# One pass for the gates and the second norm's vectors, smaller filling matmuls, and another written-out order, in a fused attention and feed-forward layer

## The chip, the cores and the metric

The kernel runs on one core of a Trainium2 chip. The core has a matrix engine (TensorE, in the profile PE, with its weight loads shown apart as PEld), a vector engine (VectorE, DVE), an activation engine (ScalarE, ACT), a general engine (GpSimd, POOL) and a queue engine (SyncE, SP) that issues most transfers. Work memory is SBUF; matmuls write to PSUM. The metric is the device time of one execution in microseconds (us); lower is better. The kernel before takes 171.2 us, the median of three runs (170.99 to 171.49).

## The reference

The input x has 2048 rows of 448 values. A small vector c gives six modulation vectors of 448 values; attention is local: a row looks at 8 earlier rows, two apart, in 16 heads of 28 values.

```
mod = silu(c) @ w_mod                       # 448 -> 6 x 448
sa, ca, ga, sb, cb, gb = mod
h = layernorm(x) * (1 + ca) + sa
x = x + ga * (local_attention(h, wqkv) @ wo)
h = layernorm(x) * (1 + cb) + sb
x = x + gb * (silu(h @ w1) @ w2)            # 448 -> 1792 -> 448
```

So the first norm needs sa and ca as soon as it runs. The gate ga is needed when the product with wo is formed (the kernel multiplies it into wo), sb and cb with the second norm, gb before the product with w2.

## The kernel before, in words

The 2048 rows go through in four chunks of 512 rows (`NC = 4`), 256 of each parity (`CP = 256`). For chunk k the steps are: first norm (`n1.k`), its transposition and modulation (`T`, `mod`), projection to queries and keys in four groups (`QKk.i.g`), to values (`Vb`), logits `Lb.par`, exponentials `exp`, masks, the product with the values `AVb`, its normalisation `onorm`, a transposing transfer `oTb`, the output projection `WOk.i`, the second norm `n2.k`, and the two feed-forward products `F1.k.i` and `F2.u`. Nine blocks b of 112 positions carry the attention.

Most products of 448 deep sums are cut in halves of 64 partitions, two of which run in the array at a time (`halves`, `duo`); a product therefore comes in two pieces of 6 and 8 matmuls, with a "turn" on POOL between.

Every step is an operation of a class `Plan`. `Plan` can order them itself by costs, but the fast path does not: `ORDER` is a long string of operation numbers, written out by hand or by a search, with a letter where an operation may run on ACT (`a`) or DVE (`v`). Operations are issued in exactly this order, and each engine runs its own ones in this order. The semaphores follow from the buffers that are shared. The scarce buffer is PSUM: four slots (`ps`) of two banks each. Two engines that read the same slot are put one behind the other.

The pieces that matter here:

- `warm_up` (L403): matmuls on a tile of zeros (`junk`) that nobody reads. Eight come first (`WARM`), then five pairs (`JUNK`), spread between the first transposes.
- `mod_cols` (L423): modulation vectors as columns, for one norm: 32 matmuls with a single moving column (L433), then two small DVE copies to `modc` (L436, L437). It is called for sa and ca (the first norm), and again for sb and cb (the second).
- `gate` (L443): one gate, spread over all 128 partitions: four matmuls of 448 columns (L450) with `screp`, which is silu(c) repeated 128 times (L421), then a copy to `gbc` (L453, ACT in this order). It is called for ga and for gb.
- `wo*g` (L879) multiplies ga into wo on DVE; two transfers on SP (L882, L883) then copy the halves of wo across partitions; the output projections wait for them. `w2*g` (L884) multiplies gb into w2 in seven steps.
- `Norm.on_pe` (L520): the first chunk's two half norms (`n1.00`, `n1.01`) are transposed on PE. Each takes one PSUM slot, four transposes per row tile (L529) and two modulation operations of two instructions each (L536 on ACT, L538 on DVE).
- `pad` (L564, L566): spreads the loaded weights of queries and keys, four operations.
- The loads of w_mod are issued in parts: columns 0 to 2D early, then 2D to 3D, 3D to 5D and 5D to 6D, each as two transfers.

The order on PE from the first values to the second output projection is, in names (a name that comes twice is a product's two pieces):

```
V0 V0 V1 L1.0 V1 QK1.0.1 QK1.0.0 L1.1 ... QK1 ... AV0 gate AV1 L2.0 V2 V2 V3 L2.1 V3
QK2.0.0 QK2.0.2 L3.0 QK2.0.0 QK2.0.2 AV2 WO0.0 L3.1 WO0.0 QK2.0.3 QK2.0.1 V5 ... AV3 V5 WO0.1
... QK3 ... WO1.0 V6 ... QK3.0.3 V8 QK3.0.3 mods gate AV4 F1.0.6 ...
```

Of the kernel before, what the change touches and what calls it, by code (L numbers as in the profile page):

```python
# [7 lines left out]
BF16 = mybir.dt.bfloat16  # L8
# [7 lines left out]
D = 448  # L16
# [4 lines left out]
KT = 4  # L21
K3 = D - 384
SP_ = 1024
# [13 lines left out]
WARM, JUNK = 8, 5  # L37
# [204 lines left out]
def layer(ctx, tc, io, safe):  # L242
# [45 lines left out]
    maskb = ct([128, 2, 128], "maskb")  # L288
    c4, sc4 = (both[0:KT, KT * 6 * D + 1024 + 128 * a:KT * 6 * D + 1152 + 128 * a] for a in range(2))
    scT = ct([128, KT], "scT")  # L290
    screp = ct([128, KT, 128], "screp")
    scratch = (both[:, KT * 6 * D + 512:KT * 6 * D + 512 + D], wqk3[:])
    modc = ct([128, 4, KT], "modc", F32)
    gbc = ct([128, 2, D], "gbc")
# [704 lines left out]
```

## Time and profile before

| | |
|---|---|
| median of the runs | 171.2 us (170.99 to 171.49) |
| the profiled execution | 171.64 us, of which the span of instructions is 169.9 us |
| PE busy | 162.0 us (95% of the span) |
| ACT busy | 114.5 us (67%) |
| DVE busy | 96.1 us (57%) |
| POOL busy | 33.2 us (20%) |
| transfers | 17.51 MB |

The span runs from the first to the last instruction; about 1.7 us of the execution lie around it. Times of the traces count from the span's start. A matmul row's duration is its whole passage through the array, and neighbours overlap: the distance between starts, which the chain of waits shows as time over count, is what a matmul costs in a stream.

### The profile page before, as it was taken

What the parts mean: (1) busy time and instruction counts of PE and PEld (TensorE: products, weight loads), DVE (VectorE), ACT (ScalarE), POOL (GpSimd) and SP (SyncE); (2) the same over time, 40 slices, a digit from 0 to 9 for tenths busy, and PEclk for the clock granted to TensorE, in tenths of its full rate; (3) what the DMA queues carried; (4) which work ended last, traced back from release to release, by engine and by line L of the source; (5) the groups of instructions that cost most, each with busy time, mean ns of one, the idle gap of its engine ahead of it and who ended that gap; (6) DMA issues with size and microseconds to landing.
All of it is one profiled execution on the core that took longest, in us unless ns stands there. A gap on an engine that the chain in (4) does not pass through costs nothing.

```text
span 169.9 us, 4812 instructions
## 1 busy us (share of the span) xinstructions
PE 162.0 (95%) x2015; PEld 83.9 (49%) x2015; DVE 96.1 (57%) x189; ACT 114.5 (67%) x163; POOL 33.2 (20%) x88
## 2 busy tenths in 40 slices
PE   7799999899999999999999999999999999999990
PEld 2258644545554564455644544655544444445450
DVE  4777999899979963895352577732473000000451
ACT  3148999999876889999878998662767862420000
POOL 7342424730502221132000205120150000000000
PEclk9959999999999999999999999999999999999999
DMA  4994448489979874022020030086008000000031
GB/s 142 289 326 165 99 94 314 78 202 242 176 185 252 177 198 106 0 66 46 20 54 0 4 90 22 2 112 178 6 10 224 0 4 0 0 4 0 38 136 64
DMA packets 32054, 17.51 MB, mean 103 GB/s; under 512 B 23896, under 2 KB 31640, under 8 KB 32024
## 3 DMA queue, kind: packets, MB, share of 16 engines
q1 hardware_dynamic: 31872, 16.90, 39.9%
q8 instruction: 17, 0.28, 0.7%
q10 hardware_dynamic: 152, 0.23, 0.5%
q14 instruction: 13, 0.11, 0.2%
HBM read 9.12 MB, written 1.84 MB: 64 GB/s over the span
## 4 chain that ended last, share of the span: by engine, by line
PE 75%; ACT 10%; DMA 6%; issue 3%; DVE 2%; POOL 1%; ACTq 0%; POOLq 0%
PE ps L791 25%; PE ps L808 22%; PE ps L627 7%; PE ps L753 6%; PE ps L638 5%; ACT p L678 4%; PE ps L730 4%; DMA wqk<-in_A_wqkv_dram 3%; PE ps L832 3%; PE ps L670 3%; DMA x_all<-in_A_x_dram 2%; ACT h L536 2%; ACT qk L630 1%; POOL rs L487 1%; ACT both L480 1%
## 5 line engine op out<-in xcount | busy, mean ns | idle before, releaser
L791 PE MATMUL ps<-h,w 64*128 64x512 bf16 x392 | 44.7, 376 | 0.0
L808 PE MATMUL ps<-w,both 64*128 64x448 bf16 x392 | 39.9, 349 | 0.0
L794 ACT ACTIVATE both<-ps 128x1024 bf16<-128x1024 f32 x28 | 27.3, 1023 | 13.9 <-PE ps L791 13.8
L678 ACT ACTIVATE p<-ps 128x896 bf16<-128x896 f32 (+1 forms) x36 | 31.5, 928 | 3.3 <-PE ps L670 3.2
L791 PEld LDWEIGHTS <-w 64*128 64x128 bf16 x392 | 19.5, 94 | 21.6
L808 PEld LDWEIGHTS <-both 64*128 64x128 bf16 x392 | 18.9, 94 | 17.7
L823 DVE TENSOR_TENSOR ot<-ps,x_all 128x896 bf16<-128x896 f32 x7 | 7.6, 1088 | 34.6 <-PE ps L808 34.3
L627 PE MATMUL ps<-h,wp 64*128 64x256 bf16 (+1 forms) x224 | 20.4, 323 | 0.6 <-ACT h L536 0.4
L627 PEld LDWEIGHTS <-wp 64*128 64x128 bf16 x280 | 13.9, 94 | 11.3 <-issue 1.1
L704 DVE TENSOR_TENSOR p<-p,maskb 128x1792 bf16<-128x1792 bf16 (+1 forms) x18 | 19.3, 1098 | 0.0
L768 DVE SCALAR_TENSOR_TENSOR x_all<-ps,x_all 128x448 bf16<-128x448 f32 x16 | 9.3, 618 | 9.7 <-PE ps L753 9.7
L487 POOL TENSOR_TENSOR rs<-rs,negh 128x2 f32<-128x2 f32 x16 | 13.8, 861 | 1.3
L753 PE MATMUL ps<-wo,oT 64*128 64x448 bf16 x112 | 13.0, 350 | 0.0
L480 ACT ACTIVATE wqk<-x_all,mv 128x448 bf16<-128x448 bf16 x16 | 10.7, 667 | 3.2 <-POOL mv L477 3.0
L477 POOL TENSOR_SCALAR mv<-sums 128x2 f32<-128x2 f32 x10 | 4.8, 479 | 40.0 <-DVE x_all L768 22.2
L638 PE MATMUL ps<-wv,h 64*128 64x448 bf16 x98 | 11.3, 350 | 0.2
L557 DVE TENSOR_SCALAR h<-h,modc 128x512 bf16<-128x512 bf16 x19 | 6.8, 408 | 6.6 <-DMA h<-xn 6.6
L630 ACT CAST qk<-ps 128x1024 bf16<-128x1024 f32 (+1 forms) x12 | 10.0, 871 | 0.7 <-PE ps L627 0.7
L321 ACT ACT_TABLE_LOAD x8 | 10.3, 1283 | 0.1
L486 POOL TENSOR_SCALAR rs<-mv 128x2 f32<-128x2 f32 x10 | 3.6, 356 | 33.3 <-ACT wqk L480 14.5
L736 DVE TENSOR_TENSOR o<-ps,rc 112x896 bf16<-112x896 f32 (+1 forms) x9 | 9.8, 1091 | 0.4
L501 DVE TENSOR_SCALAR xn<-x_all,mv,rs 128x512 bf16<-128x512 bf16 x23 | 8.8, 406 | 1.7 <-POOL rs L487 1.7
(84 smaller groups left out, 161.8 us busy)
## 6 DMA issues: line engine op xcount, KB each, us to landing
out_dram<-ot SPq DMA_DIRECT2D x7, 224.0 KB, 2.2
both<-in_w_mod_dram SPq DMA_DIRECT2D x2, 672.0 KB, 6.0
x_all<-in_A_x_dram SPq DMA_DIRECT2D x3, 448.0 KB, 7.0
w<-in_B_w_dram SPq DMA_DIRECT2D x3, 448.0 KB, 4.2
w<-in_B_w_dram SPq DMA_DIRECT2D x1, 896.0 KB, 5.3
both<-in_w_mod_dram SPq DMA_DIRECT2D x2, 336.0 KB, 5.8
w<-in_B_w_dram SPq DMA_DIRECT2D x1, 672.0 KB, 5.4
wqk<-in_A_wqkv_dram SPq DMA_DIRECT2D x1, 448.0 KB, 5.7
```

The source lines that it names most:

```text
L321: P.load = lambda t: S.preload_act_table(ACTF.Exp if t == "e" else ACTF.Silu)
L480: S.activation(out=scratch[late], in_=x_all[:, us[j], :], func=ACTF.Square, bias=mv[:, j, 0:1], accum_out=mv[:, j, 1:2])
L487: G.tensor_tensor(out=rs[:, j:j + n], in0=rs[:, j:j + n], in1=negh[:, 0:n], op=ALU.pow)
L627: return T.matmul(ps[:, j, 0:2 * n], lhsT=w.rearrange("p h d -> p (h d)"), rhs=h[rows, :, t, c0:c0 + n], start=start, stop=stop)
L630: copy_on(o)(out=qk[:, :, g, :, s0:s0 + n], in_=ps[:, :, 0:2 * n].rearrange("p j (t s) -> p j t s", t=2))
L638: return T.matmul(ps[:, j, 0:D], lhsT=h[rows, j, t, b0:b0 + 128], rhs=wv[rows, t, :], start=start, stop=stop)
L678: S.activation(out=out_, in_=ps[:, :, 0:4 * nq].rearrange("p j (g q) -> p j g q", q=nq), func=ACTF.Exp, scale=SCALE)
L704: V.tensor_tensor(out=p, in0=p, in1=maskb[:, 1 if b == 0 else 0, 0:nq].unsqueeze(1).to_broadcast([128, H, nq]), op=ALU.mult)
L753: return T.matmul(box["ps"][:, j, 0:D], lhsT=oT[rows, j, kk, s0:s0 + 128], rhs=wo[rows, j, kk, :], start=start, stop=stop)
L791: return T.matmul(ps[:, j, :], lhsT=w, rhs=h[rows, :, t, :], start=start, stop=stop)
L794: S.activation(out=hid[:, k % 2, :, i, :], in_=ps[:], func=ACTF.Silu)
L808: return T.matmul(box["ps"][:, par, 0:D], lhsT=hid[rows, k % 2, f % 2, f // 2, 128 * (2 * i + par):128 * (2 * i + par) + 128], rhs=w2[rows ...
```

## The change

- **Gates and second norm's vectors.** `gate` and the second call of `mod_cols` go. `gates` computes the four vectors ga, sb, cb, gb in one pass ("rows"): 16 matmuls of 448 columns, each with 32 weight columns, so that vector v lands in the 32 partitions from 32v; four such column groups fill the array. `screp` is 32 instead of 128 wide. ACT copies the result to SBUF ("grow"). Then two matmuls spread ga and gb over 128 partitions ("gate", by a constant matrix `avg` of 1/32, which a new fill on DVE makes at the start), and eight with one moving column turn sb and cb into columns ("mods"). One copy on DVE writes both gates to `gbc`; two small ones write `modc`. Both gates and the vectors now come at one place, behind the whole of w_mod, which is loaded in two parts (2D to 4D, 4D to 6D) instead of three: 6 transfers of w_mod in all instead of 8.
- **Filling matmuls.** `JUNK` is 12 single matmuls instead of 5 pairs. Eight of them stand directly behind the first eight; before, two pairs did.
- **First transposes.** `n1.00` takes two PSUM slots, one bank of each; each of its two modulation operations reads one slot. `n1.01` takes one bank of one slot, and one operation of four instructions on ACT modulates it.
- **Order.** `ORDER` is another list throughout. Some operations change engine: to DVE go the copies of QK0.1.1, QK2.0.1, V2, halo2, gbc and scT, two norm steps of n1.3, two of n2.1 and one each of n2.2 and n2.3, two modulations of n2.2 and one of n2.3; to ACT go the copies of QK2.0.3, QK3.0.1, V3, V4 and halo1, one norm step of n1.2, two modulations of n1.3 and one of n2.1.

On SP, the 448 KB load of the query and key weights goes ahead of its two 56 KB ones; the load of x for the last chunk moves from before the values' weights to behind the transposing transfers of n1.1; the second 672 KB load of w_mod stands between the two transposing transfers of n1.2.

On PE the same stretch as above now reads:

```
V1 V0 L1.0 V1 V0 QK1.0.3 L1.1 ... QK1 ... AV0 QK1.0.2 AV1 V2 L2.0 V2 rows V3 L2.1 gate V3
QK2.0.0 L3.0 QK2.0.0 V5 QK2.0.2 AV2 QK2.0.2 V5 QK2.0.1 L3.1 QK2.0.1 QK2.0.3 V4 QK2.0.3 V4 AV3 WO0.0 L4.0 WO0.0 WO0.1 WO0.1
QK3.0.1 mods QK3.0.0 ... WO1.0 ... AV4 V8 F1.0.6 ...
```

On DVE, from the first modulation to `wo*g`, before and after:

```
before: n1.00 mod, pad, 4 n1.1 stat, QK0.0.2, 2 n1.1 norm, QK0.1.0, 2 n1.1 norm, n1.2 stat, QK0.1.2, halo1, n1.3 stat,
  n1.2 stat, QK0.1.3, 4 n1.1 mod, V1, mask1.0, mask0.0, n1.2 norm, n1.3 stat, n1.2 norm, mask0.1, mask1.1, 2 n1.2 norm,
  onorm0, onorm1, wo*g, 4 n1.2 mod
after: n1.00 mod, pad, 4 n1.1 stat, 2 n1.1 norm, QK0.0.2, 2 n1.1 norm, QK0.1.0, QK0.1.3, 2 n1.2 stat, QK0.1.2, QK0.1.1,
  screp, 4 n1.1 mod, V1, 2 n1.2 norm, mask0.0, mask1.0, mask0.1, 2 n1.3 stat, n1.2 norm, mask1.1, onorm0, onorm1,
  2 n1.3 norm, V2, 4 n1.2 mod, gbc, mask2.0, halo2, mask2.1, QK2.0.0, wo*g, onorm2, 2 n1.3 norm, mask3.0, mask3.1
```

The diff, with the string cut out:

```
-WARM, JUNK = 8, 5
+WARM, JUNK = 8, 12
...
-    screp = ct([128, KT, 128], "screp")
+    screp = ct([128, KT, K32], "screp")
+    avg = ct([128, 128], "avg")
...
+    V.memset(avg, 1.0 / K32)
...
-    ld_mo, ld_mb, ld_m2 = load_mod(2 * D, 3 * D, late), load_mod(3 * D, 5 * D, late), load_mod(5 * D, 6 * D, late)
+    ld_mr = load_mod(2 * D, 4 * D, late) + load_mod(4 * D, 6 * D, late)
...
-        junks.append(P.op(("pe", 431.0), lambda o: warm_up(w_last, 2), [w_last] + junks[-1:], mode="f", name="junk"))
+        junks.append(P.op(("pe", 216.0), lambda o: warm_up(w_last, 1), [w_last] + junks[-1:], mode="f", name="junk"))
...
+    def gates():
+        box = {}
+        def at(v):
+            return slice(K32 * v, K32 * v + K32)
         def mm(o):
+            box["r"] = bank(o)[:, 0, 0:D]
             for k in range(KT):
+                for v in range(4):
+                    T.matmul(box["r"][at(v)], lhsT=screp[:, k, :], rhs=wmod[:, k, (2 + v) * D:(3 + v) * D], start=(k == 0), stop=(k == KT - 1))
+        def every(o):
+            box["g"] = bank(o)
+            for i, v in ((0, 0), (1, 3)):
+                T.matmul(box["g"][:, i, 0:D], lhsT=avg[at(v)], rhs=junk[at(v), 0:D], start=True, stop=True)
+        def cols(o):
+            box["c"] = bank(o)
+            for j in range(KT):
+                for i, v in ((0, 1), (1, 2)):
+                    T.matmul(box["c"][:, i, j:j + 1], lhsT=junk[at(v), ROW[j]:ROW[j] + 128], rhs=avg[at(v), 0:1], start=True, stop=True)
+        def ev(o):
+            V.tensor_copy(out=modc[:, 2, :], in_=box["c"][:, 0, 0:KT])
+            V.tensor_scalar(out=modc[:, 3, :], in0=box["c"][:, 1, 0:KT], scalar1=1.0, scalar2=None, op0=ALU.add)
+        a = P.op(("pe", 850.0), mm, [rep] + ld_mr, take=("ps",), mode="c", name="rows")
+        r = P.op(either(430.0, 540.0), lambda o: copy_on(o)(out=junk[:, 0:D], in_=box["r"]), [a] + junks, give=((a, "ps"),), name="grow")
+        e = P.op(("pe", 230.0), every, [r], take=("ps",), mode="q", name="gate")
+        c = P.op(("pe", 150.0), cols, [r], take=("ps",), mode="q", name="mods")
...
-                    box["ps"] = bank(o)[:].rearrange("p a n -> p (a n)").bitcast(BF16).rearrange("p (a n) -> p a n", a=2)
+                    box["ps"] = [pst[o["slot"][s]][:, 0, :].bitcast(BF16) for s in slots]
...
-            self.done = [P.op(either(540.0, 450.0), lambda o, a=a: mod(o, a), trs + list(waits) + self.after, name=tag + " mod") for a in range(2)]
+            t = either(1020.0, 725.0) if apart else either(1930.0, 1350.0)
+            self.done = [P.op(t, lambda o, a=a: mod(o, a), trs + list(waits) + self.after, give=((trs[0], s),), name=tag + " mod") for a, s in enumerate(slots)]
...
-            g_o = gate(0, 2, ld_mo)
-            g_2 = gate(1, 5, ld_m2)
-            mod2 = mod_cols((3, 4), 2, ld_mb)
-            wmod_read.append(mod2)
+            g_o, mod2 = gates()
+            g_2 = g_o
```

More of the change, by code (lines that the diff above doesn't have):

```diff
@@ L22 @@
 K3 = D - 384
+K32 = 32
 SP_ = 1024
@@ L420, in layer @@
     sc_op = P.op(either(210.0, 75.0), lambda o: copy_on(o)(out=scT[:], in_=box["c"]), [a], give=((a, "ps"),), name="scT")
-    rep = P.op(("dve", 310.0), lambda o: V.tensor_copy(out=screp[:], in_=scT[:].unsqueeze(2).to_broadcast([128, KT, 128])), [sc_op], name="screp")
+    rep = P.op(("dve", 110.0), lambda o: V.tensor_copy(out=screp[:], in_=scT[:].unsqueeze(2).to_broadcast([128, KT, K32])), [sc_op], name="screp")
     def mod_cols(vecs, dst0, loads):
@@ L441, in layer @@
     wmod_read = []
-    def gate(i, v, loads):
+    def gates():
         box = {}
+        def at(v):
+            return slice(K32 * v, K32 * v + K32)
         def mm(o):
-            box["ps"] = bank(o)[:, 0, 0:D]
+            box["r"] = bank(o)[:, 0, 0:D]
             for k in range(KT):
-                T.matmul(box["ps"], lhsT=screp[:, k, :], rhs=wmod[:, k, v * D:(v + 1) * D], start=(k == 0), stop=(k == KT - 1))
-        a = P.op(("pe", 757.0), mm, [rep] + loads, take=("ps",), mode="f", name="gate")
-        wmod_read.append(a)
-        return P.op(either(430.0, 540.0), lambda o: copy_on(o)(out=gbc[:, i, :], in_=box["ps"]), [a], give=((a, "ps"),), name="gbc")
+                for v in range(4):
[16 more added lines that the diff above has]
+        c = P.op(("pe", 150.0), cols, [r], take=("ps",), mode="q", name="mods")
+        wmod_read.extend([a, e, c])
+        g = P.op(either(act_ns(2 * D), dve_ns(2 * D)), lambda o: copy_on(o)(out=gbc[:], in_=box["g"][:, :, 0:D]), [e], give=((e, "ps"),), name="gbc")
+        return g, P.op(("dve", 150.0), ev, [c], give=((c, "ps"),), name="modc")
     mod1 = mod_cols((0, 1), 0, ld_ma)
@@ L539, in on_pe @@
             for j in range(2):
-                trs.append(P.op(("pe", 234.0), lambda o, j=j: tr(o, j), [self.nr[j]] + (trs[-1:] or self.after), take=() if j else ("ps",),
+                trs.append(P.op(("pe", 234.0), lambda o, j=j: tr(o, j), [self.nr[j]] + (trs[-1:] or self.after), take=() if j else slots,
                                 give=((self.nr[0], "xn"),) if j else (), mode="f", name=tag + " T"))
-            self.done = [P.op(either(540.0, 450.0), lambda o, a=a: mod(o, a), trs + list(waits) + self.after, name=tag + " mod") for a in range(2)]
-            P.op(("none", 0.0), none, self.done, give=((trs[0], "ps"),))
+            t = either(1020.0, 725.0) if apart else either(1930.0, 1350.0)
+            self.done = [P.op(t, lambda o, a=a: mod(o, a), trs + list(waits) + self.after, give=((trs[0], s),), name=tag + " mod") for a, s in enumerate(slots)]
         def on_dma(self, dst, out_of, vec, waits):
```

15 lines of the change are left out of this document (8 added, 7 removed), and 42 rows, old and new, of the table ORDER.

## The prediction

> **What bounds the kernel now.** I read the page first, then the chain of waits, then windows over it. On the page:
>
> ```profile
> span 169.9 us, 4812 instructions
> PE 162.0 (95%) x2015; PEld 83.9 (49%) x2015; DVE 96.1 (57%) x189; ACT 114.5 (67%) x163; POOL 33.2 (20%) x88
> PE 75%; ACT 10%; DMA 6%; issue 3%; DVE 2%; POOL 1%; ACTq 0%; POOLq 0%
> ```
>
> PE is busy almost throughout and has three quarters of the chain. The windows show where it is not alone (start:end, then busy time of PE, PEld, DVE, ACT, POOL, the granted clock, the DMA share and GB/s):
>
> ```profile
> 9.50:10.80 1.30, 1.30 (x12) 1.09 (x13) 1.20 (x6) 0.14 (x1) 0.91 (x3) 0.50 0.97 293
> 10.80:12.70 1.90, 1.90 (x7) 0.54 (x5) 1.44 (x5) 1.71 (x3) 0.00 (x0) 0.50 1.02 374
> 11.70:37.65 25.95, 24.70 (x391) 14.41 (x391) 23.11 (x49) 25.03 (x41) 10.29 (x21) 0.98 0.60 164
> 12.70:37.84 25.14, 23.89 (x391) 14.36 (x392) 22.76 (x48) 24.31 (x41) 10.29 (x21) 1.00 0.58 156
> 37.84:166.00 128.16, 127.96 (x1560) 64.96 (x1556) 64.32 (x116) 86.55 (x119) 16.60 (x35) 1.00 0.35 79
> ```
>
> There are two stages. From 37.84 to the last matmul PE stands still for 0.20 us in all (128.16 less 127.96): here a matmul taken away is time saved. From 12.7 to 37.84 PE, DVE and ACT are all busy 90% and more, and PE has 1.25 us to spare: here the latest of three queues decides. The chain of waits (start, us, what) gives the places:
>
> ```profile
> 4.97 5.66 DMA wqk<-in_A_wqkv_dram
> 11.79 2.85 ACT h L536 x6
> 37.84 1.29 PE ps L627 x12
> 39.13 0.33 PE ps L670 x16
> 41.30 0.90 PE ps L730 x32
> 42.20 0.86 PE ps L753 x8
> 51.72 0.76 PE ps L638 x8
> 60.92 0.88 PE ps L433 x32
> 61.80 0.78 PE ps L450 x4
> 150.61 9.84 PE ps L808 x104
> 160.57 5.42 PE ps L832 x28
> ```
>
> 37.84 is where QK2.0.0 begins, the third chunk's first projection; from there on the chain is nearly all PE, so I take it as the anchor: time of the anchor plus PE's work behind it. L433 and L450 at 60.92 and 61.80 are the second norm's vectors and the second gate. The last two rows give the price of a 448-column matmul: 9.84/104 = 0.095 us where halves run in pairs, 5.42/28 = 0.194 us alone on the whole array.
>
> **The change part by part.** *Work behind the anchor.* Gone are 0.88 (L433) and 0.78 (L450). L3.0, 0.33 by the L670 row, now stands ahead of the anchor. New are eight one-column matmuls ("mods"), at 0.88/32 = 0.0275 each 0.22. Net: -1.77 us. Nothing hides these, since PE waits for nothing there; that PE stays fed is an assumption I price below.
>
> *Work ahead of the anchor, on PE.* The first gate goes (0.78). "rows" comes: 16 matmuls of 448 columns on a quarter of the columns each. The trace has no matmul of this shape. If four run at once, 4 x 0.194 = 0.78; if none do, 16 x 0.194 = 3.10. I take 0.78, because the nearest row, L808, shows halves of the array running two at a time without loss (2 x 0.095 = 0.19). "gate" is two matmuls, 0.19 to 0.39, and L3.0 0.33. Net +0.5 to +0.7, under PE's spare 1.25; at 3.10 it is +3.0, and about 1.7 would come through. [...]
>
> *DVE ahead of the anchor.* QK2.0.0 needs the four modulations of n1.2, which are DVE's. The groups of DVE from 11.7 to 37.7 (count, busy us, mean ns, idle before) price the queue up to there:
>
> ```profile
> L501 DVE TENSOR_SCALAR xn<-x_all,mv,rs 128x512 bf16<-128x512 bf16 x9 | 3.4, 405 | 0.6 <-POOL rs L487 0.6
> L630 DVE CAST qk<-ps 128x512 bf16<-128x512 f32 x4 | 2.7, 684 | 1.2 <-PE ps L627 1.1
> L704 DVE TENSOR_TENSOR p<-p,maskb 128x1792 bf16<-128x1792 bf16 x2 | 2.2, 1082 | 0.0
> L557 DVE TENSOR_SCALAR wqk<-wqk,modc 128x512 bf16<-128x512 bf16 x4 | 1.4, 406 | 0.0
> L642 DVE CAST v<-ps 128x896 bf16<-128x896 f32 x1 | 1.1, 1093 | 0.2 <-ACT p L678 0.2
> L736 DVE TENSOR_TENSOR o<-ps,rc 128x896 bf16<-128x896 f32 x1 | 1.1, 1091 | 0.0
> L879 DVE TENSOR_TENSOR wo<-wo,gbc 128x1792 bf16<-128x1792 bf16 x1 | 1.1, 1080 | 0.0
> L735 DVE RECIPROCAL rc<-ps 128x32 f32<-128x32 f32 x1 | 0.3, 350 | 0.0
> L611 DVE COPY h<-h 128x256 bf16<-128x256 bf16 x1 | 0.2, 216 | 0.0
> ```
>
> Before the four modulations go wo\*g (1.08), one norm step (0.41, to ACT) and halo1 (0.22, to ACT); there come two norm steps of n1.3 (0.81), the copy of QK0.1.1 (0.68), that of V2 (1.09) and a narrower screp (quarter of a 0.42 us copy, 0.1 to 0.4 by its row below; I take 0.15). Sum: +1.02 us. Against that stand DVE's waits, 25.95 - 23.11 = 2.84 us in this window. The largest is 1.1 us of the QK0 copies for PE; two norm steps (0.81) now stand in front of the first of them. I take 0.7 us recovered, with 0 and 1.7 (that wait and the 0.6 for POOL) as ends.
>
> *The start.* These rows of the timeline (start, us, engine, line) carry it:
>
> ```profile
> 1.24 5.04 PE L405 MATMUL ps<-both 128*128 128x512 bf16 x12 [1.24 <-DVE both L339]
> 4.81 0.63 DVE L470 BATCH_NORM_STATS2 st<-x_all 128x6 f32<-128x448 bf16 x1 [1.65 <-DMA x_all<-in_A_x_dram]
> 8.19 0.40 PE L529 MATMUL ps<-ident,xn 128*128 128x128 bf16 x4 [1.26 <-DVE xn L501]
> 9.68 0.42 DVE L421 COPY screp<-scT 128x512 bf16<-128x512 bf16 x1
> 10.66 0.40 DVE L564 COPY wp<-wqk 128x896 bf16<-128x896 bf16 x1
> 10.97 0.72 DVE L538 TENSOR_SCALAR h<-ps,modc 128x256 bf16<-128x256 bf16 x2
> 12.73 1.59 PE L627 MATMUL ps<-h,wp 64*128 64x256 bf16 x26
> 33.10 0.56 ACT L453 CAST gbc<-ps 128x448 bf16<-128x448 f32 x1
> ```
>
> The weights of queries and keys land at 10.63 and hold up both engines' pads. Their 448 KB load now stands ahead of 112 KB; at 293 GB/s that is up to 0.38 us earlier. But DVE now does a pad, modc and another pad ahead of its modulation, so that it ends at about 11.8 instead of 11.69 (+0.1); a third pad ends near 12.2. Two PSUM slots free ACT from waiting for DVE's half (it began at 11.79, right after DVE's end), so it may begin near 11.2. The projections then start between 12.1 and 12.7, and ACT's part is 0 to 0.6 earlier. Since DVE decides the anchor, I count +0.1 only. The new fill `avg` falls into DVE's 1.65 us before the first load; without that cover it would cost at most the 0.63 of the shortest row there. Sixteen fillings at 5.04/12 = 0.42 end at 8.0, before the first transposes at 8.19, which wait for DVE; the matmul of c moves from 6.2 to 8.0, and its copy goes to DVE behind two norm steps. The vectors of the first norm then come about 0.3 later, still ahead of the pads. Without those covers it would be 0.4 per filling matmul.
>
> *The gate's way to WO0.0.* Before, wo\*g ran at 35.27. Now it waits behind n1.2's modulations and gbc (1.09 by the V row), two masks (2.16), halo2 (about 0.3) and a 1024-wide QK copy (1.2): 4.7 us in all. With the modulations ended at 38.1, wo\*g runs from about 42.8 to 43.9. The first copying transfer before:
>
> ```profile
> L882 SPq DMA_DIRECT2D wo<-wo x1: 508/508/508, 36.4 to 36.4; - x1
> DMA to landing us min/median/max: 5.3/5.3/5.3
> ```
>
> So the copies land at about 49.3. PE, from an anchor at 38.3, has QK2 (56 matmuls at 1.29/12 = 0.107, 6.0), V4 and V5 (28 matmuls at 0.095, 2.7), AV2, L3.1 and AV3 (2.1) in front of WO0.0: 49.1. DVE needs onorm2, two norm steps and two masks (1.44 + 0.81 + 2.16 = 4.4) after wo\*g for AV3's masks: 48.3, the same time. The wait is 0.2 and I count it nothing; behind it PE would queue up everything, since it keeps its order.
>
> *Queues.* SP's later x load and w_mod's second 672 KB part change places; the second waits behind the first transposing transfer of n1.2, whose norm steps now run before three masks, near 26, so it can land (6 us or so, by the page's row for these loads, next) by 34, where "rows" comes at about 34.5. Late, it would hold V3, L2.1 and the anchor. The other moved copies swap ACT for DVE behind the anchor, where each has time free (DVE 64.32 busy of 128.16, ACT 86.55).
>
> ```profile
> both<-in_w_mod_dram SPq DMA_DIRECT2D x2, 672.0 KB, 6.0
> ```
>
> ACT: "grow" replaces the first gbc, equal in size (0.56); the second gbc goes. Two small modc copies move, in a stretch where DVE waited anyway.
>
> **The sum.** Anchor: +0.1 (start) +1.02 (DVE's queue) -0.7 (waits) = +0.42. Behind it: -1.77. Together -1.35 us on the profiled execution's 171.64 us (span 169.9 and 1.7 around it), 170.3. The median of the runs is 171.2, 0.44 lower; on it I predict 169.9 us. The ends: anchor +1.12 gives 170.55, anchor -0.58 gives 168.85.
>
> **The rivals.**
> 1. *The early stage recovers fully.* The waits of 1.7 go, and the anchor comes at 37.3: 171.2 - 0.58 - 1.77 = 168.9. For it: the moved norm steps and the freed ACT. Against: ACT was busy 24.31 of 25.14 there.
> 2. *The saved PE work is given back.* Nothing is recovered and other order costs 0.8 us of waits behind the anchor (0.20 were left; any disorder adds): 171.2 + 1.12 - 1.77 + 0.8 = 171.3, no change.
> 3. *Column groups do not overlap*, so the change does not do what it says: 1.7 us come through, 169.9 + 1.7 = 171.6; half hidden by DVE, 171.0.
> 4. *The clock.* PE ran at half clock from 9.5 to 12.7, after it had stood 1.26 us before 8.19. The single filling matmul left before the projections may leave a gap and half clock after 12.7. For a stretch as long as that one (3.2 us) PE would lose 1.6, of which 0.5 hides: 171.0. Against: the same stop at 8.19 exists before. [...]
> 5. *The gate comes too late (slower).* ga is ready some 8 us later than before. If w_mod's last part, gbc's queue or the copies are late, WO0.0 holds PE. A landing 1.3 us behind PE, at 50.4, uses up the gain, and from 50.9 on the kernel is slower; with 2.2 (a second transfer of 224 KB that waits for the 0.5 us of issue and another 1.7 of the w2 load's bytes, 0.5 MB at 293 GB/s) it is 169.9 + 2.2 = 172.1. For it: before, the copies landed at 41.7, only 0.5 before WO0.0 at 42.20, and SP now has a 672 KB load of w2 right ahead of them. Against: the sums meet at 49.
>
> **Chances.** Forecast 0.45, rival 1 0.12, rival 2 0.10, rival 3 0.05, rival 4 0.05, rival 5 0.23. 0.3%, 0.5 us, is about what a measurement tells from no change: below 170.7 is faster (forecast and rival 1, 0.57), up to 171.7 the same (2, 3, 4: 0.20), above slower (0.23). The range 168.8 to 172.2 leaves out about half of rival 5 and a little of rival 1; the forecast's own range is 169.2 to 170.6.
>
> **What would show it.** Right: no L433 and no wide gate near 60; "rows" within 1.3 us; QK2.0.0 near 38.3 or earlier; no wait of PE at the first WO; PE idle behind the anchor under 0.5. Wrong: PE waiting for wo's copies or for w_mod, DVE's modulations of n1.2 after 39, half clock after 12.7, or new gaps where feed-forward pieces now stand in another order.

## The result, and the profile after

The changed kernel took 171.31 us (median of 20 runs), the kernel before 171.37 us beside it (20 runs): a ratio of 1.0002, 95% interval 0.9983 to 1.002. Ratios and intervals here leave out executions in which the chip ran in a slower state, so they need not be the quotient of the medians. Nothing was gained that can be measured, where 169.9 us and a gain were forecast. The profiled execution took 171.33 us (171.64 before).

The page of the changed kernel, its span, its engines and the shares of its chain of waits:

```profile
span 169.6 us, 4789 instructions
PE 161.0 (95%) x2002; PEld 82.2 (48%) x2003; DVE 97.4 (57%) x196; ACT 111.8 (66%) x157; POOL 30.6 (18%) x88
PE 62%; ACT 10%; DVE 10%; DMA 8%; issue 5%; SPq 1%; POOL 1%; DVEq 0%; ACTq 0%; POOLq 0%
```

PE has 1.0 us less work, as meant, and yet the span is only 0.3 us shorter. The chain says why in outline: PE's share fell from 75% to 62%; DVE rose from 2% to 10%, transfers from 6% to 8%, and time in which nothing shown is waited for from 3% to 5%. PE now waits for others more often. The windows (start:end, then busy time of PE, PEld, DVE, ACT, POOL, the granted clock, the DMA share and GB/s) put the waits in their stages:

```profile
9.50:10.80 1.30, 1.25 (x15) 0.80 (x13) 1.19 (x6) 1.19 (x2) 0.48 (x2) 1.00 1.05 387
10.80:12.70 1.90, 1.87 (x28) 1.47 (x28) 1.17 (x4) 1.90 (x5) 0.00 (x0) 1.00 1.06 324
11.03:36.59 25.56, 24.48 (x402) 14.56 (x403) 23.97 (x51) 24.55 (x41) 8.60 (x20) 1.00 0.75 186
36.59:165.06 128.47, 127.48 (x1534) 63.31 (x1531) 65.02 (x120) 84.19 (x113) 15.64 (x36) 1.00 0.32 76
```

36.59 is the start of QK2.0.0, the anchor of the prediction, 1.1 us earlier than before. Behind it PE stands still for 128.47 - 127.48 = 0.99 us, where it was 0.20. That counts only what the busy time shows: a matmul's end is modelled, and short stops between pieces hide in it. So I also take the time from the first matmul of each piece to the first of the next, from QK2.0.0 to the first feed-forward piece, F1.0.6. Before, this stretch took 25.62 to 25.84 us (four traces, see below), after 25.93 and 25.90, although gate and vectors (0.75 and 0.81) have gone from it and only 0.18 came. (Some tenths come and go with the moment at which the stage begins: the order of before behind the new start took 26.02, 25.98 and 25.36 us, in runs told below.) Sorted by kind, before (its second further trace) against after: logits 1.26 and 2.33, output projections 4.11 and 4.74, projections QK 11.41 and 11.24. The saved 1.4 us came back in the times of L and WO, that is, as waits.

The chain of waits of the changed kernel has their causes (start, us, what):

```profile
15.58 0.69 DVE qk L659
16.31 0.46 PE ps L699 x16
35.19 1.29 DVE wqk L586 x4
43.88 4.50 DMA h<-xn
49.12 1.10 DVE o L765
50.27 0.95 PE ps L782 x8
51.31 0.76 PE ps L782 x6
53.35 1.14 POOL mv L504
56.07 0.91 ACT qk L659
57.02 0.37 PE ps L699 x14
```

At 50.27 WO0.1 waits for onorm3 on DVE (L765, a PSUM slot comes free), which stands behind a modulation that waited for a transposing transfer (43.88). At 57.02 the logits L4.1 wait for ACT's copy of QK3.0.1 (L659), which stands behind four squares of the second norm, the last two of which waited for POOL's mean (53.35). The timeline shows the size of this one, and the other steps of the prediction (start, us, engine, line):

```profile
1.24 6.01 PE L408 MATMUL ps<-both 128*128 128x512 bf16 x16 [1.24 <-DVE both L341]
11.03 1.73 PE L656 MATMUL ps<-h,wp 64*128 64x256 bf16 x23
33.65 0.94 PE L458 MATMUL ps<-both,screp 128*32 128x448 bf16 x16
34.52 0.74 PE L667 MATMUL ps<-wv,h 64*128 64x448 bf16 x6
40.74 1.08 DVE L906 TENSOR_TENSOR wo<-wo,gbc 128x1792 bf16<-128x1792 bf16 x1
42.40 0.60 SPq L910 DMA_DIRECT2D wo<-wo  x1
48.30 0.93 PE L782 MATMUL ps<-wo,oT 64*128 64x448 bf16 x8
57.02 0.37 PE L699 MATMUL ps<-qk 28*128 28x112 bf16 x14 [0.75 <-ACT qk L659]
```

The pass ("rows", L458) starts at 33.65 and the next piece at 34.52: 16 matmuls in 0.87 us, 0.054 each, four at a time. wo\*g runs at 40.74, the second copy is issued at 42.40 and lands 3.1 us later, and WO0.0 starts at 48.30 without a wait.

The one trace of before turned out to be a late execution of its kernel: its first statistics, which wait for the first load of x, began at 4.81 us, in all other traces of this study at 3.91 to 4.49. So I took three more traces of it. The marks of all (us; "close" is from the end of the last matmul to the end of the span):

| trace | first projection | first logits | QK2.0.0 | F1.0.6 | last matmul ends | close |
|---|---|---|---|---|---|---|
| before | 12.73 | 17.52 | 37.68 | 63.30 | 165.97 | 3.94 |
| before, three more | 12.19, 11.25, 11.20 | 16.80, 16.91, 16.86 | 36.95, 37.07, 37.02 | 62.63, 62.84, 62.86 | 165.30, 165.51, 165.53 | 4.02, 4.01, 3.96 |
| changed | 11.03 | 16.31 | 36.59 | 62.52 | 165.05 | 4.55 |
| changed, again | 10.75 | 15.76 | 36.04 | 61.94 | 164.47 | 4.76 |
| changed start alone, twice | 10.91, 10.51 | 16.05, 15.66 | 36.21, 35.81 | 62.23, 61.79 | 164.90, 164.46 | 4.01, 5.26 |
| changed, old start, twice | 11.13, 11.96 | 16.66, 16.81 | 36.60, 36.74 | 62.78, 62.58 | 165.31, 165.10 | 4.54, 4.77 |

With means over the rows of before and of the changed kernel: the first logits come 0.99 us earlier; from there to QK2.0.0 0.12 is lost (20.16 before, 20.28 after, the same within 0.01 in all traces of a kernel); from there to F1.0.6 0.19 is lost; behind it 0.14 is gained; and the close is 0.67 longer. Sum: -0.15 us. In these means the start gained a microsecond, the saved PE work nothing, and the close took two thirds of it back. The start's term is partly luck: the first statistics began at 4.51 on average before and at 4.20 after, and they differ by more than that between executions of one kernel (4.49 and 3.91 in the changed one). Counted from them, the first logits come after 12.37 to 12.72 us before and 11.82 and 11.86 after, about 0.7 us sooner. Without the late trace of before, the start's term is -0.82 and the sum -0.03.

### The profile page after: what moved, and what is told of

It is laid out like the page before. It is cut to its first block, busy times and chain, and to the rows that moved or that the text cites. A ratio compares the mean times of both kernels' runs of the same rounds, so it can differ in the third digit from the quotient of the medians.

```text
span 169.6 us, 4789 instructions
## 1 busy us (share of the span) xinstructions
PE 161.0 (95%) x2002; PEld 82.2 (48%) x2003; DVE 97.4 (57%) x196; ACT 111.8 (66%) x157; POOL 30.6 (18%) x88
## 3 DMA queue, kind: packets, MB, share of 16 engines
HBM read 9.12 MB, written 1.84 MB: 65 GB/s over the span
## 4 chain that ended last, share of the span: by engine, by line
PE 62%; ACT 10%; DVE 10%; DMA 8%; issue 5%; SPq 1%; POOL 1%; DVEq 0%; ACTq 0%; POOLq 0%
PE ps L820 25%; PE ps L837 22%; DMA x_all<-in_A_x_dram 6%; PE ps L782 5%; ACT p L707 4%; PE ps L861 3%; DMA h<-xn 3%; PE ps L759 3%; ACT qk L659 2%; PE ps L699 2%; PE ps L667 2%; DVE st L497 1%; DVE o L765 1%; DVE v L671 1%; ACT both L501 1%
## 5 line engine op out<-in xcount | busy, mean ns | idle before, releaser
L656 PE MATMUL ps<-h,wp 64*128 64x256 bf16 (+1 forms) x224 | 21.0, 323 | 0.1
L504 POOL TENSOR_SCALAR mv<-sums 128x2 f32<-128x2 f32 x10 | 4.2, 423 | 58.1 <-PE ps L820 33.8
L528 DVE TENSOR_SCALAR xn<-x_all,mv,rs 128x512 bf16<-128x512 bf16 x28 | 10.2, 407 | 4.8 <-POOL rs L514 4.8
L514 POOL TENSOR_TENSOR rs<-rs,negh 128x2 f32<-128x2 f32 x16 | 12.1, 758 | 1.3
L659 ACT CAST qk<-ps 128x1024 bf16<-128x1024 f32 (+1 forms) x12 | 10.4, 902 | 2.8 <-PE ps L656 2.8
L765 DVE TENSOR_TENSOR o<-ps,rc 112x896 bf16<-112x896 f32 (+1 forms) x9 | 9.8, 1092 | 0.3
L699 PE MATMUL ps<-qk 28*128 28x112 bf16 (+1 forms) x288 | 7.5, 211 | 1.8 <-ACT qk L659 0.7
```

What stands on the lines that cost most here:

```text
L514: G.tensor_tensor(out=rs[:, j:j + n], in0=rs[:, j:j + n], in1=negh[:, 0:n], op=ALU.pow)
L656: return T.matmul(ps[:, j, 0:2 * n], lhsT=w.rearrange("p h d -> p (h d)"), rhs=h[rows, :, t, c0:c0 + n], start=start, stop=stop)
L659: copy_on(o)(out=qk[:, :, g, :, s0:s0 + n], in_=ps[:, :, 0:2 * n].rearrange("p j (t s) -> p j t s", t=2))
L699: T.matmul(held[t][:, j, g * nq:(g + 1) * nq], lhsT=key, rhs=q, start=True, stop=True)
L765: V.tensor_tensor(out=bass.AP(ot.tensor, ot.offset, [list(ot.ap[0]), [512 + K3, 2], [DH, H], [1, DH]]), in0=ps[0:nq, :, :, 0:DH], in1=r.un ...
```

## The experiments

The ratios are to the kernel before, run beside each.

**The changed kernel again.** No edit.

> The changed kernel once more, for a second trace of it beside the kernel before. Theory A (the 0.9 us of matmul time saved and the 1.7 us earlier start of the first projections are given back by matmuls that wait elsewhere and by a longer close): the same picture in the trace, first projections near 11.0, first wait at the second output projection near 50 and at L4.1 near 56, and a time within 0.5 us of before. Rival B (the early start is luck of the clock in one execution): the first projections start between 11.5 and 12.7 this time and the matmuls there run at half clock.

Measured: 171.59 us, ratio 1.0011 (0.9983 to 1.0038). The first projection is early again (10.75) and the waits are the same: L4.1 waits 0.74 us for ACT. I took the early start for proved by this. That was too soon, since it was the trace of before that was unusual; the later runs put its size right.

**Wide gates in the places of the pass.**

```diff
-            g_o, mod2 = gates()
-            g_2 = g_o
+            g_o = gate(0, 2, ld_mr)
+            g_2 = gate(1, 5, ld_mr)
+            mod2 = mod_cols((3, 4), 2, ld_mr)
+            wmod_read.append(mod2)
```

> One part undone: the changed kernel with the two wide gates and the 32 matmuls for the second norm's vectors in place of the single pass, at the same places of the order. The matmul engine has about 0.9 us more to do. If that engine alone sets the end (the prediction's view), the time is 0.9 us over the changed kernel's, about 172.2. Theory A: it fills waits that are there anyway, and DVE is relieved of 1.1 us, so at most +0.4 us.

Measured: 171.45 us, 0.9991 (0.9962 to 1.002), against 1.0011 of the changed kernel beside it. From its trace I read only the work, by distances of starts: 1.71 us for the two gates and 0.81 for the vectors, where the changed kernel has 0.87 for "rows", 0.33 for "gate" and 0.18 for "mods". That is 1.1 us of PE more in all. Ahead of the anchor it is less (the first gate, 0.86, against 1.20), and behind it 1.5 more (0.85 and 0.81 against 0.18). This PE time behind the anchor cost nothing that can be measured, where I had reckoned it one for one. DVE's wide copy of both gates is gone in this kernel too, so the run does not show the waits alone.

**The changed start alone.** The kernel before, with twelve single filling matmuls, the first transposes in two slots of PSUM, and the changed order up to the first projection.

```diff
-WARM, JUNK = 8, 5
+WARM, JUNK = 8, 12
...
-        junks.append(P.op(("pe", 431.0), lambda o: warm_up(w_last, 2), ...
+        junks.append(P.op(("pe", 216.0), lambda o: warm_up(w_last, 1), ...
...
-        def on_pe(self, out_of, waits):
+        def on_pe(self, out_of, waits, apart):
```

> One part alone: the kernel before, its order kept from the first projection on, with the changed kernel's start (single filling matmuls, two slots for the first transposes, the weights' load first, the order up to the first projection). Theory A: the first projections start near 11 us instead of 12.7, but DVE and ACT behind them do not follow in full, since they wait for the next load of x; 0.3 to 1.0 us faster than before, 170.4 to 171.1. Rival C (the start's gain is all kept, and the changed kernel loses it only later): 1.5 to 1.7 us faster, near 169.7.

Measured: 170.76 us, 0.9941 (0.9911 to 0.9971). Once more:

> The kernel with the changed start alone once more, as it was 0.9941 in the run of that name and 0.9997 with its three small loads in one. If the start is worth 1 us: 0.992 to 0.996, close 4.0 us. If the first measurement was luck: 0.997 to 1.001.

Measured: 171.01 us, 0.9956 (0.9931 to 0.9981). The start alone makes the kernel about half a per cent faster, 0.8 to 1.0 us. The part of the change that I had put at +0.1 us is the only one that gains. Fillings, slots, loads and order of the start were not run apart. ACT's rows show one piece of it (start, us); in a trace of before with full clock, whose first statistics began at 4.42:

```profile
11.18 2.84 ACT L536 ACTIVATE h<-ps,modc 128x256 bf16<-128x256 bf16 x6 [0.71 <-DVE h L538]
```

and in the changed kernel's first trace, where they began at 4.49:

```profile
10.45 2.84 ACT L565 ACTIVATE h<-ps,modc 128x256 bf16<-128x256 bf16 x6
```

Before, ACT's modulations wait 0.71 us for DVE's, with which they share a slot. In two slots they run beside them, 0.73 us earlier: the wait is gone. That this makes most of the start's gain is argued from these rows; the two slots alone were not run.

**The logits L4.0 behind the first piece of WO0.1.** Order alone.

```diff
-WO0.0 (first piece), L4.0, WO0.0 (second), WO0.1 (first)
+WO0.0 (first piece), WO0.0 (second), WO0.1 (first), L4.0
```

> The changed kernel with the logits L4.0 moved behind the first piece of WO0.1. Theory A says that WO0.1 waits there because the four PSUM slots are held by AV3, WO0.0 and the two of L4.0. With the move this wait of about 0.6 us goes; the exponentials of block 4 come up to 1 us later. If the second norm's chain (x1, squares, transposing transfer, F1.0) sets the pace, 0.3 to 0.6 us faster than the changed kernel; if it does not, no change.

Measured: 171.0 us, 0.9981 (0.9949 to 1.0012). The logits' sum fell from 7.10 to 6.70, the output projections' rose from 11.56 to 11.86, and the last matmul ends at 164.54 (164.47 in the changed kernel's second trace). The wait moved by one piece. The time is not clear of that of the kernel before, nor of the changed one.

**Eight loads instead of six.**

```diff
-    ld_mr = load_mod(2 * D, 4 * D, late) + load_mod(4 * D, 6 * D, late)
+    ld_mr = [load(672, wmod[:, 0:3, c0:c0 + 2 * D], ...) for c0 in (2 * D, 4 * D)]
+    ld_mr += [load(56, wmod[half(1), 3, c0:c0 + D], ...) for c0 in (2 * D, 3 * D, 4 * D, 5 * D)]
```

> The changed kernel, with the modulation weights in eight transfers instead of six: the two small ones (rows 384 to 447) are cut in two each, 56 KB a piece. The output's last store then falls on the same pair of completion semaphores as in the kernel before (the transfers take eight of them in turn). Theory A (the longer close, 4.55 to 4.76 us after the last matmul against 3.94 and 4.01, hangs on which of the semaphores the last stores use): the close is 3.9 to 4.1 us again, the last matmul stays within 0.2 us of 164.5, and the time falls by 0.5 to 0.7 us, to about 0.996 of the kernel before. Theory B (the close is longer for another reason, the order of the last stores or the code itself): close 4.5 or more, time 1.000 to 1.001.

Measured: 171.47 us, 0.9995 (0.9961 to 1.0028); close 4.41 us. And the other way round, in the kernel with the start alone:

```diff
-    ld_mo, ld_mb, ld_m2 = load_mod(2 * D, 3 * D, late), load_mod(3 * D, 5 * D, late), load_mod(5 * D, 6 * D, late)
+    ld_small = load(224, wmod[half(1), 3, 2 * D:6 * D], w_mod[384:D, 2 * D:6 * D], late, ...)
+    ld_mo, ld_mb, ld_m2 = ([load(...), ld_small] for c0, c1 in ((2 * D, 3 * D), (3 * D, 5 * D), (5 * D, 6 * D)))
```

> The kernel of the run with the changed start alone, with its three small loads of modulation weights (rows 384 to 447) in one, so that there are two transfers fewer, as in the changed kernel. Nothing else is changed; the loads are needed 20 us later. Theory A (the close hangs on which completion semaphores the last stores use): the close becomes 4.5 to 4.8 us instead of 4.01, and the time 0.997 to 0.998 of the kernel before, where the changed start alone gave 0.9941. Theory B: close 4.0, time 0.994.

Measured: 171.36 us, 0.9997 (0.9963 to 1.0031); close 4.64 us, against 4.01. The number of loads does change the close in this direction, but my reason covers only a part. In SP's instructions at the end of the traces there are two pieces. First, SP waits for eight semaphores in a fixed order; before, the last store used the last of them, and in the changed kernel two more waits stand behind it, 0.13 us. With eight loads this piece is gone. Second, a gap of 0.38 to 0.39 us in SP's last instructions is in the changed kernel, with six loads and with eight, and in the kernel with the start alone and six loads; it is in none of the four traces of before and in neither of the start alone. What makes the gap stays open. The 5.26 us of the start alone's second trace are another matter: there the last store took 3.05 us from issue to landing, 1.84 to 1.92 in the traces of before, and from its landing to the end it is 1.52 us, against 1.41 before and 1.97 in the changed kernel. In time the two runs cannot settle it: the start alone with six loads is 0.4 to 0.6% above the two runs without that edit, the way theory A says, the changed kernel with eight loads 0.1% below, and the intervals overlap.

**Four fillings instead of twelve.**

```diff
-WARM, JUNK = 8, 12
+WARM, JUNK = 8, 4
```

> The changed kernel without eight of its twelve single filling matmuls: the ones that run straight behind the first eight are left out, the four that stand between the first transposes and the projections stay. Theory A (the early clock comes from the fillings keeping PE busy from 1.2 to 7.3): PE stands still from about 4.7, the granted clock shows half speed for some 3 us after the first transposes near 9, the first projection begins 0.5 to 1.5 us later than 10.8 to 11.0 or runs at half clock, and the first logits come 0.5 to 1.5 us later than 15.8 to 16.3; the time rises by 0.3 to 1.0 us. Theory B (the early start comes from the order of the loads and the two slots alone): first projection by 11.1, no half clock after it, time unchanged.

Measured: 172.46 us, 1.0037 (1.0003 to 1.0071). The first logits come at 17.43, the last matmul ends at 165.93. The windows show the clock (column before the last two):

```profile
7.00:9.50 2.50, 2.00 (x41) 1.84 (x42) 1.91 (x8) 0.34 (x1) 2.03 (x6) 0.58 1.05 343
9.50:12.70 3.20, 3.20 (x20) 1.79 (x20) 2.69 (x11) 2.66 (x6) 0.12 (x1) 0.50 1.08 324
12.70:16.80 4.10, 4.10 (x64) 3.36 (x62) 2.38 (x8) 3.20 (x7) 1.71 (x6) 0.81 0.51 129
```

Without the early fillings PE is in this trace at half clock from 7.4 to 14.2 us (0.58 as a mean of full and half in the first row, 0.81 in the last), some 7 us, and the first logits come 1.1 to 1.7 us later than in the changed kernel. In time the fillings' worth is not clear: 1.0037 is above the changed kernel's 1.0002 and 1.0011, but the intervals overlap.

**The groups of the pass in turn.**

```diff
-            for k in range(KT):
-                for v in range(4):
+            for v in range(4):
+                for k in range(KT):
```

> The changed kernel with the pass over the four column groups issued group by group (four matmuls of one group, then the next group's four) instead of one matmul of each group in turn: the same 16 matmuls. If the 0.87 us of the pass come from four column groups running at one time, they now take about 16 x 0.194 = 3.1 us, 2.2 more, and as PE has about 1 us or less to spare ahead of the third chunk's first projection, that comes 1.0 to 2.2 us later, the time 1.006 to 1.013. If a quarter-wide matmul is short by itself, the pass stays at 0.9 us and the time does not move.

Measured: 171.67 us, 1.0009 (0.9971 to 1.0047); the pass takes 0.90 us (33.59 to 34.49):

```profile
33.59 0.97 PE L458 MATMUL ps<-both,screp 128*32 128x448 bf16 x16
34.49 0.74 PE L667 MATMUL ps<-wv,h 64*128 64x448 bf16 x6
```

Neither slower nor what I expected of overlap. Either a quarter-wide matmul is short by itself, or the groups overlap whatever order they are issued in. One more run decides that.

**The first group four times over.**

```diff
-            for k in range(KT):
-                for v in range(4):
+            for v in (0, 0, 0, 0, 1, 2, 3):
+                for k in range(KT):
```

> The changed kernel with the first column group's four matmuls issued four times over (16 on the same 32 columns, one behind the other) and then the other three groups' four each: 28 matmuls instead of 16. If a quarter-wide matmul of 448 columns is short by itself, the pass takes 28 x 0.054 = 1.5 us. If matmuls on the same columns follow each other at the 0.194 us of a whole one, and the groups overlapped even when issued in turn because several can be under way, it takes 16 x 0.194 = 3.1 us or more.

Measured, in PE's timeline:

```profile
33.82 3.24 PE L458 MATMUL ps<-both,screp 128*32 128x448 bf16 x28
37.00 0.74 PE L667 MATMUL ps<-wv,h 64*128 64x448 bf16 x6
39.05 0.82 PE L656 MATMUL ps<-wqk,wp 64*128 64x512 bf16 x6
```

28 matmuls take 3.18 us, which is 16 x 0.194 (3.10) for the first group with the other twelve beside it. A quarter-wide matmul is as long as a whole one (3.18/16 = 0.199 us against 0.194); the groups run at one time, also when they are written in turn. And the 2.31 us that were added came through in full: QK2.0.0 is at 39.05 instead of 36.59, and the one execution took 173.79 us (the kernel before beside it: 171.86). The stops of PE in this stage could hide none of it. In the changed kernel they all lie before 24.5 us, as its windows show:

```profile
11.03:24.50 13.47, 12.39 (x212) 8.66 (x214) 12.01 (x30) 12.82 (x22) 4.30 (x13) 1.00 0.80 207
24.50:36.59 12.09, 12.09 (x192) 5.90 (x191) 11.95 (x22) 11.73 (x20) 4.29 (x7) 1.00 0.70 164
```

**The old start in the changed kernel.** The pass and the rest of the order stay; fillings, slot and order up to the first projection are those of before (the start's edits reversed).

> The changed kernel with the start of the kernel before: five pairs of filling matmuls, the first transposes in one slot of PSUM, and the order before up to the first projection; the pass over four column groups and the rest of the order stay. Theory A (the start gains about 1 us, and the rest of the change costs as much): first projection near 12.7, third chunk's first projection 37.0 to 37.9, last matmul 165.3 to 166.0, time 172.0 to 172.6, 1.004 to 1.007 of the kernel before. Theory B (start and rest are each worth nothing that can be measured): 0.998 to 1.002. The forecast on record would have given 0.992 for the rest alone.

Measured: 171.57 us, 0.9996 (0.9966 to 1.0026); first logits 16.66, QK2.0.0 36.60, last matmul 165.31, close 4.54. Theory B's range, and the first projection was at 11.13 at full clock with the old start: this showed that the trace of before had misled me. That the start is worth nothing, as theory B says, holds for the changed kernel only: ahead of the old order it was measured twice at half a per cent. Here the old start brings the first logits about 0.7 us later, and QK2.0.0 and the last matmul about 0.4 later (means of two traces each, with the next run), and the time shows none of it. Once more:

> The changed kernel with the old start once more. If the old start brings half clock in most executions whatever the rest is: granted clock 0.5 between 9.5 and 12.7 and first projection at 12.2 to 12.8. If the rest of the change (a narrower repeat of the vector, one small fill more on DVE, other loads behind the first ones) keeps the clock up with the old start as well: 1.0, and first projection at 11.0 to 11.4 as in its first trace.

Measured: half clock from 9.5 to 12.7, first projection 11.96, first logits 16.81, last matmul 165.10, 171.60 us. The three further traces of before:

> The kernel before, unchanged, for a second trace of it. If the half clock and the late projection belong to the kernel: granted clock 0.5 between 9.5 and 12.7, first projection at 12.2 to 12.8, third chunk's first projection at 37.2 to 37.8. If they belong to the one execution: full clock, first projection at 11.0 to 11.6, third chunk's first projection near 36.5, last matmul near 164.7.

> The kernel before once more, as in the run ahead of this: a third trace of it, with the same two expectations.

> The kernel before once more: a fourth trace of it, with the same two expectations.

Their times were 171.06, 171.34 and 171.22 us. One has half clock, two have not. The first of them, in windows:

```profile
9.50:10.80 1.30, 1.08 (x10) 0.81 (x10) 1.30 (x7) 0.72 (x1) 0.81 (x3) 0.50 1.01 372
10.80:12.70 1.90, 1.90 (x13) 0.74 (x14) 1.36 (x5) 1.64 (x4) 0.00 (x0) 0.65 1.06 390
```

and the second:

```profile
9.50:10.80 1.30, 0.99 (x10) 0.63 (x11) 1.30 (x7) 0.94 (x1) 0.25 (x1) 1.00 0.97 356
10.80:12.70 1.90, 1.64 (x16) 0.70 (x16) 1.87 (x5) 1.52 (x4) 0.00 (x0) 1.00 1.06 390
```

Both reach the first logits at the same time, 16.80 and 16.91. With the old start the half clock belongs to the execution, not to the kernel, and costs nothing here, also when counted from the first statistics (12.37 us with it, 12.49 and 12.48 without): at full clock PE only waits longer, for ACT. The start's gain, read at the first logits, is 16.66 to 16.91 (17.52 in the late trace) against 15.66 to 16.31. The rest of the change, by the means of its two traces against the four of before, ends the last matmul 0.37 us earlier and closes 0.67 later.

**Three moves against the waits.** Order alone, in the changed kernel.

```diff
-DVE: ..., n1.1 norm, QK0.0.2 copy, ...      n1.3 mod, onorm3, ...   mask4.0, halo3, n2.0 norm
+DVE: ..., QK0.0.2 copy, n1.1 norm, ...      onorm3, n1.3 mod, ...   mask4.0, QK3.0.1 copy, halo3, n2.0 norm
-ACT: n2.0 squares, QK3.0.1 copy, QK3.0.0 copy
+ACT: n2.0 squares, QK3.0.0 copy
```

> The changed kernel with three moves in its order, each at a place where PE stood still in its trace: the copy of QK3.0.1 goes from ACT (where it stood behind four squares of the second norm and held L4.1 for 0.74 us) to DVE, behind mask4.0; onorm3 goes ahead of n1.3's modulation on DVE (it held a PSUM slot that WO0.1 waits for); the copy of QK0.0.2 goes ahead of two norm steps of n1.1 on DVE (it held L0.0). Theory A (the 0.94 us of PE work that the change saves go into waits that its other order makes behind the third chunk's first projection): sums of L and WO fall by 0.7 to 1.3 us together, the last matmul comes at 163.2 to 163.9 instead of 164.5, time 0.993 to 0.996. Theory B (a wait taken away comes back at the next place, as when L4.0 was moved): last matmul within 0.3 of 164.5, time 0.999 to 1.001.

Measured: 171.15 us, 0.9961 (0.993 to 0.9993). The stretch from QK2.0.0 to F1.0.6 in windows, before (its second further trace):

```profile
37.07:62.84 25.77, 25.66 (x386) 13.52 (x384) 22.59 (x43) 21.14 (x35) 5.60 (x12) 1.00 0.92 200
```

the changed kernel:

```profile
36.59:62.52 25.93, 25.02 (x358) 12.51 (x357) 21.86 (x44) 21.61 (x33) 6.32 (x13) 1.00 0.82 184
```

and with the three moves:

```profile
36.70:61.59 24.89, 24.68 (x359) 12.50 (x357) 22.30 (x43) 20.55 (x32) 5.46 (x13) 1.00 0.85 174
```

PE stands still 0.91 us in the second and 0.21 in the third, and the stretch is 1.0 us shorter. So most of the saved PE work had gone into these waits: for the stretch that is shown. But it is not kept. Ahead of the stretch the three moves lose 0.39 (20.67 us from the first logits to QK2.0.0 against 20.28). PE reaches the feed-forward sooner and meets a wait that it did not have, in the waits between 87 and 123 us:

```profile
PE ps L782 <- DMA oT<-o: 0.5, 1, 0.5
```

Of the 1.0 us, 0.15 is lost by F2.0 and 0.67 more between 87 and 123 us, and 0.2 are left from QK2.0.0 to the end of the last matmul; from the first logits on, nothing is gained. The last matmul ends at 164.96, within neither theory's range. Whether the kernel with the moves is faster than the changed one itself cannot be told by these intervals; that it is faster than the kernel before is at the edge of its own. The start alone remains the best version measured twice.

## Why the prediction was wrong, step by step

| term | forecast, us | measured, us |
|---|---|---|
| start, up to the first logits | +0.1 | -0.99 |
| DVE's queue less waits, to QK2.0.0 | +0.32 | +0.12 |
| behind the anchor, to F1.0.6 | -1.77 | +0.19 |
| behind F1.0.6 | 0 | -0.14 |
| close | 0 | +0.67 |
| sum | -1.35 | -0.15 |

The last column holds differences of means, the late trace of before among them.

**The step that failed is "Nothing hides these, since PE waits for nothing there", with its assumption "that PE stays fed".** It put the whole PE saving behind the anchor, -1.77 us, into the time. PE's work behind the anchor did fall, by 0.75 + 0.81 - 0.18 = 1.38 us (I had 1.77: the logits L3.0 do not stand ahead of QK2.0.0 but behind its first piece, so their 0.33 stays). But the time from the anchor to F1.0.6 did not fall; it rose by 0.19. The 0.20 us of stops before is a property of that order, not of the stage: the changed order puts onorm3 behind a late modulation and the copy of QK3.0.1 behind the second norm's squares, and PE loses 1.6 us (1.38 and 0.19) to waits. The run with wide gates and that with the three moves show it from both sides: 1.5 us of PE work added behind the anchor costs nothing measurable, and taking waits away brings 1.0 us of stretch. Where the other half microsecond waits, no run shows. This is rival 2 (the saved work is given back), with twice the 0.8 us of waits that I gave it. That its time, 171.3, is what came is luck: it had the anchor 1.12 us later, which came 0.87 earlier by the means, and it did not have the longer close.

**The start** was mis-sized in the other direction. A mechanism was named (two slots free ACT from DVE's half, the load of the weights comes earlier), but I let DVE decide the anchor and counted +0.1. From the first logits to QK2.0.0 every trace of before takes 20.16 us, with the start alone too, so a shift of the logits passes through whole in that order. In the changed order it does not: with the old start this way takes 19.93 us, with the new one 20.28. ACT's modulations, not DVE's, stood last in front of the logits before. I also took the anchor from a late execution: 37.68, where three others have 36.95 to 37.07.

**The close** was not in the sum at all. By itself it is half of the gain that was forecast.

**Right.** "rows" was 0.87 us against 0.78 forecast, far from 3.10; four column groups give 0.194/0.054 = 3.6 times the speed of one. No run shows the 1.3 us that is named as the bound for "rows"; the pass stayed below it. DVE's queue to the anchor was right within 0.2, but its parts were not: DVE's work from the first projection to QK2.0.0 grew by 1.02 us, as reckoned, from 22.95 in the second further trace of before (next row) to 23.97, and its waits fell from 2.87 to 1.59, by 1.28 where I had taken 0.7.

```profile
11.25:37.07 25.82, 24.22 (x389) 14.42 (x390) 22.95 (x49) 24.99 (x41) 10.31 (x21) 1.00 0.61 162
```

The way of the gate to WO0.0 held: wo\*g at 40.74 (42.8 forecast), copies landed at 45.5 (49.3; the transfers took 3.1 us instead of 5.3), WO0.0 at 48.30 (49.1), no wait, so that rival 5 fell. w_mod's second part was there when "rows" began. The fillings ended at 7.25 (8.0), and no half clock followed in either trace of the changed kernel (granted 1.00 from 9.5 to 12.7), so rival 4 did not come; the half clock that I priced there at 1.6 us of PE cost nothing in the kernel before. Rival 3 (groups do not overlap) fell. Rival 1 (the early stage recovers fully) came for the anchor, at 36.0 to 36.6 against 37.3, mostly by the start.

**PE's "spare 1.25 us" ahead of the anchor** was not spare where the pass stands: its stops lie before 24.5 us. Nothing followed from it here, since the pass cost 0.87, but 2.31 us more in that place came through whole.

## What to carry to other kernels

Before a saving on the busiest engine is counted one for one, ask who feeds the pieces that move up: an order written out by hand is tight only for the durations it was written for, and the second-latest release becomes the wait. A sum against one trace inherits that execution's luck; marks that are constant between traces of one order (here 20.16 us from the first logits to QK2.0.0) are the ones to add terms to. When a change holds several edits, price the smallest ones with the same care: here the changed start, put at +0.1 us, carried all of the gain.

## What the runs showed of the hardware that was not expected

Matmuls on different column groups run at one time even when the kernel writes them group by group: 16 of 448 columns in 0.90 us in turn and 0.87 interleaved, while 16 on the same group, with twelve on the other three beside them, take 3.18. For the groups in turn I had expected 3.1 us (16 x 0.194), if the overlap hung on the interleaved order. In the trace of that run the matmuls do not start in the order in which the kernel writes them: the one that waits for the second part of w_mod, ninth as written, is the third to start, 0.03 us after the first. Whether the engine changed the order, or the building of the program before it, no run shows.

Half clock at the start is there in two of the four traces of the same kernel (0.50 granted between 9.5 and 10.8) and absent in two (1.00). By the clock records of the two it lasted 3.41 us, from 9.30 and from 8.73; with four fillings it lasted 6.83 us. With the old start three of six traces have it; with twelve fillings it is in one of eleven, that of the wide gates, from 10.03. It cost nothing where PE waited for ACT anyway (first logits at 16.80 us with it, at 16.91 and 16.86 without); with four fillings, where it lasted longest, the first logits came 1.1 to 1.7 us later, though how much of that is the clock was not measured apart.

The close of the program, from the last matmul to the end of the span, was 3.94 to 4.02 us in four traces of one kernel and 4.41 to 4.77 in the traces of the changed kernel and its variants, but for the wide gates: 6.43, where the last store took 3.77 us to land. 0.13 of the difference is the place of the last store's semaphore among eight that are waited for in turn; 0.39 is a gap on SP whose cause is open.
